# State exponentials and 1/rms without TensorE transposes: VectorE block transposes and DMA in a fused attention and feed-forward kernel

## The chip, the core and the metric

The kernel runs on one core of a Trainium2 chip. A core has a matrix engine (TensorE, "PE" in the profile, with its weight loads as "PEld"), VectorE (DVE), ScalarE (ACT), GpSimd (POOL), a queue engine that issues transfers (SyncE, "SP" or "SPq"), and 16 DMA engines that carry them. The metric is the time of one execution on the device in microseconds, lower is better. The kernel before takes 791.16 us, the median of three runs between 791.04 and 791.2.

## What is computed

Two blocks follow one another. The first is a cross attention between 512 tokens and 32 state vectors, for 8 batches and 8 heads of width 64, in both directions: tokens read from states and states read from tokens. The second is a gated feed-forward layer on all 8 x 544 rows, with a normalization by the root of the mean square (rms) ahead of it. The reference, cut to what matters:

```python
# x: (8, 8, 512, 64)   state: (8, 8, 32, 64)
scores = scale * x @ state.T ;  a  = softmax(scores)       # 512 x 32 for each head
xread  = a @ state                                          # the tokens' rows
scores2 = scale * state @ x.T ; a2 = softmax(scores2)       # 32 x 512 for each head
sread  = a2 @ x                                             # the states' rows
y = concatenate([xread, sread], axis=2)  ->  rows (8*544, 512)
rms = sqrt(mean(y*y, -1) + 1e-6)
yn  = y / rms * rms_g                                       # rms_g: 512 numbers
out = (silu(yn @ w_gate) * (yn @ w_val)) @ w_out            # 512 -> 1536 -> 512
```

All is float32.

## The kernel before

The batches are worked in periods. While TensorE does the two feed-forward products of batch b, the attention of batch b+1 is done beside and between them. Each piece of work is a generator, which yields after every step; one string gives the order in which the generators are stepped, and TensorE, VectorE and ScalarE run their instructions in just this order. Transfers go out on the SyncE queue, in the order in which the program issues them, and SyncE waits at each for whatever that transfer needs.

```python
PERIOD = (
    "hhtvtvhtxhuxhuthhtuhuhtxhhhutuuuhthhuttxahhxhthuuuuuxhavuvhtxhtxhhttuauhxuxhxuut"
    "hhhtuhthutuuhuuuhhauuhtaaauxuhthautuuhhthuhuautaaphuuuapuaaaaacaasapcpaaaaaaaakp"
    "psackaauaacakkpapaakaacpsaskcsssppsasspwswkswxkxxkkpxpxccxss"
)
# h: products to the hidden layer   t, u: their copies (ScalarE) and sums (VectorE)
# p: products of the second layer   c, k: their copies and sums, with the stores
# a: tokens_read(b+1)               s: states_read(b+1)
# w, v: own weights of a batch, two of them for b+1, with the next 1 MB of weights fetched
```

The attention weights of the next batch come from `tokens_read`. Its last steps find 1/rms of each token and scale the weights by it:

```python
    def mean_root(ss, n):
        ri = two.tile([P, NC], F32, name="ri")
        GE.tensor_tensor(out=ri[:, 0:n], in0=ss, in1=mhalf[:, 0:n], op=ALU.pow)     # line 270
        return ri

    def along_rows(ri, n):
        rp = aps.tile([P, NC, P], F32, name="at")
        for c in range(n):
            TE.transpose(out=rp[:, c, :], in_=ri[:, c:c + 1].to_broadcast([P, P]),  # line 277
                         identity=ident)
        return rp.rearrange("p c t -> p (c t)")

    def tokens_read(b):
        ...                                    # softmax over the states, and the read: line 410
        sq = one.tile([P, 4, S], F32, name="sq", tag="xT")
        for i, j in enumerate((2, 3, 0, 1)):
            SE.activation(out=sq[:, i, :], in_=reads[j], func=ACTF.Square, scale=DM ** -0.5)
            ...
        for i, j in ((0, 1), (2, 3), (0, 2)):
            VE.tensor_tensor(out=sq[:, i, :], in0=sq[:, i, :], in1=sq[:, j, :], op=ALU.add)
            yield
        sp = aps.tile([P, NC], F32, name="at")
        for c in range(NC):                                        # NC = 4
            TE.matmul(out=sp[:, c:c + 1], lhsT=sq[:, 0, P * c:P * c + P], rhs=ones,   # line 424
                      start=True, stop=True)
        yield
        ss = two.tile([P, NC], F32, name="ss")
        VE.tensor_scalar(ss, sp, 1e-6, None, op0=ALU.add)          # line 428
        yield "step"
        ri = mean_root(ss, NC)
        yield
        rp = along_rows(ri, NC)
        yield
        VE.tensor_tensor(out=aT_s[b], in0=aT_s[b],                 # line 434
                         in1=rp.unsqueeze(1).to_broadcast([P, 2, S]), op=ALU.mult)
        yield "step"
```

The states' rows come from `states_read`. The exponentials are made with the states on partitions, and are needed with the tokens on partitions:

```python
    def states_read(b):
        ...                                                        # the maxima
        for e in range(2):
            SE.activation(out=e2[:, e], in_=sS[:, e], func=ACTF.Exp, scale=SCALE,
                          bias=s2[:, e:e + 1], accum_out=z2[:, e:e + 1])
            yield "step" if e else None
        e2T = one.tile([P, 2, NC, P], F32, name="e2T")
        for e in range(2):
            tp = aps.tile([P, NC, P], F32, name="at")
            for c in range(NC):
                TE.transpose(out=tp[:, c, :], in_=e2[:, e, c, :], identity=ident)   # line 459
            yield
            SE.copy(e2T[:, e], tp)                                 # line 461
            yield "step"
        ...
        for e in range(2):
            for c in range(NC):
                for j in range(4):
                    h = 2 * j + e
                    TE.matmul(out=rp[Ns * j:Ns * j + Ns, e, :],    # line 471
                              lhsT=e2T[:, e, c, Ns * j:Ns * j + Ns],
                              rhs=xb[:, c, D * h:D * h + D], ...)
        ...                                                        # scaled, transposed, kept
```

The products of the second layer are line 836 (fourteen steps `p` in a period, each 6 matmuls in the program, 12 in the trace, where each float32 matmul of this kind shows as two). A batch's own weights are line 528, and each of them is followed by `fetch`, which issues the load of the next 1 MB of weights. The sums `k` and copies `c` of a period also store eight tiles of 128 KB, through the same SyncE queue.

Of the kernel before, what the change touches and what calls it, by code (L numbers as in the profile page):

```python
# [8 lines left out]
F32 = mybir.dt.float32  # L9
# [3 lines left out]
ALU = mybir.AluOpType  # L13
ACTF = mybir.ActivationFunctionType
AXX = mybir.AxisListType.X
PSUM = bass.MemoryType.PSUM

P = 128
# [10 lines left out]
)  # L29

PERIOD = (
    "hhtvtvhtxhuxhuthhtuhuhtxhhhutuuuhthhuttxahhxhthuuuuuxhavuvhtxhtxhhttuauhxuxhxuut"
    "hhhtuhthutuuhuuuhhauuhtaaauxuhthautuuhhthuhuautaaphuuuapuaaaaacaasapcpaaaaaaaakp"
    "psackaauaacakkpapaakaacpsaskcsssppsasspwswkswxkxxkkpxpxccxss"
)

STATES = (
# [6 lines left out]
def kernel(  # L44
# [20 lines left out]
    nc = tc.nc  # L65
    VE, SE, GE, TE = nc.vector, nc.scalar, nc.gpsimd, nc.tensor
# [50 lines left out]
    def load_x(b, *queues):  # L117
# [8 lines left out]
        for c in range(NC):  # L126
# [3 lines left out]

    ident = consts.tile([P, P], F32, name="ident")
    make_identity(nc, ident)
    mhalf = consts.tile([P, NC], F32, name="mhalf")
    GE.memset(mhalf, -0.5)
    ones = consts.tile([P, 1], F32, name="ones")
    GE.memset(ones, 1.0)

    GE.tensor_tensor(out=consts.tile([P, NC], F32, name="first_pow"), in1=mhalf,
                     in0=ones.to_broadcast([P, NC]), op=ALU.pow)
    bounds = consts.tile([P, 2], F32, name="bounds")  # L140
    GE.memset(bounds[:, 0:1], 1151.0 + 7.5 / 16)
    GE.memset(bounds[:, 1:2], 255.0 * (1 << 23))
    rms_g = consts.tile([P, NI], F32, name="rms_g")


    w_d = [scratch.tile([P, NI, 2, 2, P], F32, name="w_d%d" % mp) for mp in range(NM // 2)]
    w_sb = {}
    wo = consts.tile([P, NM, DM], F32, name="wo")
    hb = consts.tile([P, NM, S], F32, name="hb")
# [117 lines left out]
    def mean_root(ss, n):  # L267

        ri = two.tile([P, NC], F32, name="ri")
        GE.tensor_tensor(out=ri[:, 0:n], in0=ss, in1=mhalf[:, 0:n], op=ALU.pow)  # L270
        return ri
# [11 lines left out]
    def scores(b, packed, soft):  # L283

        xb = x_sb[b]
        stT = two.tile([P, 4, Ns], F32, name="stT")
        tp = aps.tile([P, 4, Ns], F32, name="at")
        TE.transpose(out=tp.rearrange("p j n -> p (j n)"),
                     in_=packed.rearrange("p e d -> p (e d)"), identity=ident)
        yield  # L290
        VE.tensor_copy(stT, tp)
        yield "step"

        xT = one.tile([P, 4, NC, P], F32, name="xT", tag="xT")
        for c in range(NC):
            tp = aps.tile([P, 4, P], F32, name="at")
            for j in range(4):
                TE.transpose(out=tp[:, j, :], in_=xb[:, c, P * j:P * j + P], identity=ident)
            yield
            SE.copy(xT[:, :, c, :], tp)  # L300
            yield "step"
# [12 lines left out]
        eS = soft["e"] = one.tile([P, 2, S // Ns, Ns], F32, name="eS", tag="eS")  # L314
        for e in range(2):
            VE.transpose(out=eS[:, e].rearrange("p k n -> p (k n)"), in_=sp[e])
            yield
            SE.copy(sS[:, e].rearrange("p c t -> p (c t)"), sp[e])
            yield "step" if e else None

        soft["st"] = stT
        soft["half"] = lambda e: eS[:, e]
        soft["back"] = lambda e: [(aT_s[b][:, e], eS[:, e].rearrange("p k n -> p (k n)"))]

    def scores_of_blocks(b, packed, soft):
# [30 lines left out]
        for g in (2, 3, 0, 1):  # L356
# [7 lines left out]
                                   eS[:, g].rearrange("p e c n -> p e (c n)"))  # L364
                                  for g in (2 * q, 2 * q + 1)]

    def tokens_read(b):
        packed, soft = rows.pop(b), {}
        yield from (scores if b < 2 else scores_of_blocks)(b, packed, soft)
        half = soft["half"]  # L370
        m1 = two.tile([P, 2, S // Ns], F32, name="m1")
        z1 = two.tile([P, 2, S // Ns], F32, name="z1")

        def along(t, e):
            return t[:, e].unsqueeze(2).to_broadcast([P, S // Ns, Ns])

        for e in range(2):
            VE.reduce_max(out=m1[:, e], in_=half(e), axis=AXX)
            yield
            VE.tensor_tensor(out=half(e), in0=half(e), in1=along(m1, e), op=ALU.subtract)  # L380
            yield
            SE.activation(out=half(e), in_=half(e), func=ACTF.Exp, scale=SCALE)
            yield "step"
        stT_g[b] = two.tile([P, 4, Ns], F32, name="stT_g")
        if b > 1:
            soft["st"] = aps.tile([P, 4, Ns], F32, name="at")
            TE.transpose(out=soft["st"].rearrange("p j n -> p (j n)"),
                         in_=packed.rearrange("p e d -> p (e d)"), identity=ident)
            yield
        VE.tensor_tensor(out=stT_g[b], in0=soft["st"], in1=rms_g.unsqueeze(2).to_broadcast([P, 4, Ns]),  # L390
                         op=ALU.mult)
        yield
        aT_s[b] = two.tile([P, 2, S], F32, name="aT_s")
        for e in range(2):
            VE.reduce_sum(out=z1[:, e], in_=half(e), axis=AXX)
            yield
            VE.tensor_scalar(z1[:, e], z1[:, e], 1e-9, None, op0=ALU.add)
            VE.reciprocal(z1[:, e], z1[:, e])
            yield
            VE.tensor_tensor(out=half(e), in0=half(e), in1=along(z1, e), op=ALU.mult)  # L400
            yield
            for to, blocks in soft["back"](e):
                VE.transpose(out=to, in_=blocks)
            yield "step"


        reads = [(aps, vps)[j // 2].tile([P, S], F32, name=("at", "pv")[j // 2]) for j in range(4)]
        for j in range(4):
            for e in range(2):
                TE.matmul(out=reads[j][D * e:D * e + D, :],  # L410
                          lhsT=packed[Ns * j:Ns * j + Ns, e, :],
                          rhs=aT_s[b][Ns * j:Ns * j + Ns, e],
# [5 lines that stand above are left out]
            yield "step" if i == 3 else None  # L418
        for i, j in ((0, 1), (2, 3), (0, 2)):
            VE.tensor_tensor(out=sq[:, i, :], in0=sq[:, i, :], in1=sq[:, j, :], op=ALU.add)  # L420
            yield
        sp = aps.tile([P, NC], F32, name="at")
        for c in range(NC):
            TE.matmul(out=sp[:, c:c + 1], lhsT=sq[:, 0, P * c:P * c + P], rhs=ones,  # L424
                      start=True, stop=True)
        yield
        ss = two.tile([P, NC], F32, name="ss")
        VE.tensor_scalar(ss, sp, 1e-6, None, op0=ALU.add)
        yield "step"
        ri = mean_root(ss, NC)  # L430
        yield
        rp = along_rows(ri, NC)
        yield
        VE.tensor_tensor(out=aT_s[b], in0=aT_s[b],  # L434
                         in1=rp.unsqueeze(1).to_broadcast([P, 2, S]), op=ALU.mult)
        yield "step"

    def states_read(b):

        xb, sS = x_sb.pop(b), read.pop(b)  # L440
        e2 = one.tile([P, 2, NC, P], F32, name="e2")
        s2 = two.tile([P, 2], F32, name="s2")
        m2 = two.tile([P, 2], F32, name="m2")
        z2 = two.tile([P, 2], F32, name="z2")
# [4 lines left out]
        VE.tensor_scalar(s2, m2, -SCALE, None, op0=ALU.mult)  # L449
        yield  # L450
        for e in range(2):
            SE.activation(out=e2[:, e], in_=sS[:, e], func=ACTF.Exp, scale=SCALE,
                          bias=s2[:, e:e + 1], accum_out=z2[:, e:e + 1])
            yield "step" if e else None
        e2T = one.tile([P, 2, NC, P], F32, name="e2T")
        for e in range(2):
            tp = aps.tile([P, NC, P], F32, name="at")
            for c in range(NC):
                TE.transpose(out=tp[:, c, :], in_=e2[:, e, c, :], identity=ident)  # L459
            yield  # L460
            SE.copy(e2T[:, e], tp)
            yield "step"
        VE.tensor_scalar(z2, z2, 1e-9, None, op0=ALU.add)
        VE.reciprocal(z2, z2)
        yield
# [1 line left out]
        for e in range(2):  # L467
            for c in range(NC):
                for j in range(4):
                    h = 2 * j + e  # L470
                    TE.matmul(out=rp[Ns * j:Ns * j + Ns, e, :],  # L471
                              lhsT=e2T[:, e, c, Ns * j:Ns * j + Ns],
                              rhs=xb[:, c, D * h:D * h + D],
                              start=(c == 0), stop=(c == NC - 1))
        yield
# [567 lines left out]
```

## Time and profile before

| what | value |
|---|---|
| time, median of 3 | 791.16 us |
| span of the profiled run | 789.0 us, TensorE clock granted 1.000 |
| busy share VectorE, ScalarE, GpSimd | 66%, 42%, 22% |
| share of the 16 DMA engines, SyncE's queue | 36.6% |
| one period (from one batch's line 471 to the next one's, 214.57 and 300.05 us) | 85.48 us |
| transposes of the exponentials, line 459 | 64, mean 273 ns from start to end |
| their copies on ScalarE, line 461 | 16, mean 581 ns |
| sums over partitions, line 424 | 64, mean 241 ns |
| spread of 1/rms, line 277 | 34, mean 274 ns |
| power -1/2 on GpSimd, line 270, 128 x 4 | 8, mean 1692 ns |
| scaling by 1/rms on VectorE, line 434 | 8, mean 1220 ns |

How to read it: matmuls are pipelined, so the time that one of them takes from start to end is longer than the time by which the next one follows. What a group of them costs TensorE is read from the starts in the timeline. Busy shares are averages over the span; the length is set by the engine that has no gaps.

### The profile page before, as it was taken

How to read it: one execution, taken by the hardware profiler on the slowest of the kernel's cores; microseconds unless marked ns; L12 is line 12 of the kernel's file. 1: busy time of each engine (PE TensorE's matmuls, PEld its weight loads, DVE VectorE, ACT ScalarE, POOL GpSimd, SP SyncE). 2: the span in 40 equal slices, each digit the busy share in tenths (PEclk: the TensorE clock that was granted, in tenths of full speed). 3: DMA queues.
4: the chain of work that ended last, by engine and by line, in shares of the span. 5: the costliest groups of instructions: out<-in, count | busy, mean ns of one | idle time of the engine just before them, and what ended most of it. 6: DMA issues, size and time to landing. Idle time of an engine off the chain costs nothing.

```text
span 789.0 us, 13559 instructions
## 1 busy us (share of the span) xinstructions
PE 776.5 (98%) x5478; PEld 603.5 (76%) x5478; DVE 521.5 (66%) x822; ACT 334.4 (42%) x560; POOL 170.9 (22%) x216
## 2 busy tenths in 40 slices
PE   6999999999999999999999999999999999999998
PEld 5643444788877887888878887788788887888996
DVE  4999997688338951897168833895189715781461
ACT  5998864552245323542255224532354225410320
POOL 0100003430244023410433024402341043400000
PEclk9999999999999999999999999999999999999999
DMA  9788865730075005610263008400530034201311
GB/s 286 226 287 298 276 191 167 217 122 1 25 239 181 2 18 181 227 22 17 102 206 121 1 26 257 163 2 15 201 154 7 14 106 149 108 7 34 121 54 27
DMA packets 69277, 95.77 MB, mean 121 GB/s; under 512 B 46432, under 2 KB 54112, under 8 KB 62304
## 3 DMA queue, kind: packets, MB, share of 16 engines
q1 hardware_dynamic: 67040, 94.33, 36.6%
q8 instruction: 43, 0.70, 0.4%
q10 hardware_dynamic: 2176, 0.59, 0.4%
q14 instruction: 18, 0.15, 0.1%
HBM read 79.69 MB, written 15.20 MB: 120 GB/s over the span
## 4 chain that ended last, share of the span: by engine, by line
PE 92%; DVE 5%; DMA 1%; issue 0%; ACT 0%; SPq 0%
PE f L674 37%; PE f L836 35%; PE f L776 5%; PE pv L570 4%; PE at L528 3%; PE pv L528 3%; DVE ex L248 1%; PE at L471 1%; PE at L410 1%; DVE raw L244 1%; PE at L346 1%; PE at L459 1%; PE at L424 1%; DMA raw<-in_moe_w_gate_dram 1%; DVE w_m L253 1%; PE pv L346 1%
## 5 line engine op out<-in xcount | busy, mean ns | idle before, releaser
L836 PE MATMUL f<-wo,hb 128*128 128x256 f32 x540 | 123.4, 380 | 0.2 <-ACT ot L873 0.2
L674 PE MATMUL f<-aT_s,v 128*128 128x256 f32 x504 | 120.6, 382 | 0.0
L836 PEld LDWEIGHTS f<-wo,hb 128*128 128x128 f32 x540 | 101.4, 190 | 13.6 <-ACT ot L873 0.4
L674 PEld LDWEIGHTS f<-aT_s,v 128*128 128x128 f32 x504 | 94.1, 190 | 19.6 <-DVE c L736 5.0
L736 DVE TENSOR_TENSOR g<-g,f 128x512 f32<-128x512 f32 (+1 forms) x96 | 61.8, 653 | 68.4 <-PE f L674 63.9
L674 PE MATMUL f<-aT_t,vs 128*128 128x256 f32 x336 | 87.1, 381 | 0.0
L270 POOL TENSOR_TENSOR ri<-ss,mhalf 128x4 f32<-128x4 f32 x8 | 13.5, 1692 | 320.4 <-DVE s L449 210.9
L727 ACT ACTIVATE hb<-g 128x1024 f32<-128x1024 f32 (+1 forms) x48 | 48.2, 1004 | 79.3 <-DVE g L736 79.3
L836 PE MATMUL f<-wt,hs 128*128 128x256 f32 x360 | 81.0, 381 | 0.0
L836 PEld LDWEIGHTS f<-wt,hs 128*128 128x128 f32 x360 | 67.3, 190 | 14.1 <-issue 5.1
L674 PEld LDWEIGHTS f<-aT_t,vs 128*128 128x128 f32 x336 | 63.2, 190 | 15.0 <-issue 5.9
L873 ACT COPY ot<-f 128x256 f32<-128x256 f32 x60 | 21.4, 373 | 123.0 <-PE f L836 123.0
L554 POOL TENSOR_TENSOR vs<-v 128x256 f32<-128x256 f32 x42 | 31.3, 746 | 164.2 <-ACT v L539 164.1
L739 DVE SCALAR_TENSOR_TENSOR hb<-hb,g 128x1024 f32<-128x1024 f32 x42 | 53.2, 1266 | 4.6 <-ACT hb L727 4.6
L725 ACT COPY g<-f 128x512 f32<-128x512 f32 (+1 forms) x48 | 26.9, 561 | 55.8 <-PE f L674 55.8
L776 PE MATMUL f<-wo,hb 128*128 128x512 f32 x96 | 44.7, 600 | 0.0
L557 POOL TENSOR_TENSOR vs<-v,vs 128x256 f32<-128x256 f32 x42 | 44.4, 1057 | 0.0
L570 PE MATMUL pv<-aT_s,v 128*128 128x512 f32 x96 | 43.7, 594 | 0.2 <-DVE aT_s L434 0.2
L674 PE MATMUL f<-aT_s,vs 128*128 128x256 f32 x168 | 43.1, 379 | 0.0
L674 PE MATMUL f<-aT_t,v 128*128 128x256 f32 x168 | 43.1, 379 | 0.0
L836 PE MATMUL f<-wo,hs 128*128 128x256 f32 x180 | 41.1, 379 | 0.0
L836 PEld LDWEIGHTS f<-wt,hb 128*128 128x128 f32 x180 | 33.7, 190 | 9.4 <-DVE ot L881 5.0
(144 smaller groups left out, 1277.0 us busy)
## 6 DMA issues: line engine op xcount, KB each, us to landing
w_m<-w_d SPq DMA_DIRECT2D x48, 1024.0 KB, 6.5
out_dram<-ot SPq DMA_DIRECT2D x56, 128.0 KB, 2.2
raw<-in_moe_w_val_dram SPq DMA_DIRECT2D x6, 1024.0 KB, 5.5
raw<-in_moe_w_out_dram SPq DMA_DIRECT2D x6, 1024.0 KB, 8.6
x_b<-in_x_dram SPq DMA_DIRECT2D x96, 64.0 KB, 2.8
w_d<-w_m SPq DMA_DIRECT2D x6, 1024.0 KB, 4.9
raw<-in_moe_w_gate_dram SPq DMA_DIRECT2D x5, 1024.0 KB, 7.1
x_b<-in_x_dram SPq DMA_DIRECT2D x6, 256.0 KB, 6.8
```

Source lines behind the costliest of these rows:

```text
L528: TE.matmul(out=pv[e][Ns * j:Ns * j + Ns, :], lhsT=stT_g[b][D * e:D * e + D, j, :], rhs=w[D * e:D * e + D, j].rearrange("p m k f -> p (m k ...
L554: GE.tensor_tensor(out=vs[:, 0], in0=a21, in1=a22, op=ALU.add)
L557: GE.tensor_tensor(out=vs[:, 2], in0=a12, in1=vs[:, 1], op=ALU.subtract)
L570: TE.matmul(out=to[0], lhsT=lhs(i, k), rhs=r, start=(i == 0), stop=(i == len(rhs) - 1))
L674: TE.matmul(out=ps[:, i, 0:half], lhsT=l[:, i, :], rhs=r, start=(start and i == 0 and k == 0), stop=(k == len(lhs) - 1), skip_group_check= ...
L725: SE.copy(gates(q)[1], q["x"][:, :, 0:half])
L727: SE.activation(out=hb[:, 2 * mp:2 * mp + 2, 0:n].rearrange("p m (c t) -> p m c t", c=2), in_=q["g"][:, :, :, 0:half], func=ACTF.Silu if s ...
L736: VE.tensor_tensor(out=to, in0=to, in1=q[ps][:, :, 0:half], op=ALU.add)
L739: VE.scalar_tensor_tensor(out=h, in0=h, scalar=1.0, op0=ALU.add, op1=ALU.mult, in1=q["g"].rearrange("p m c t -> p m (c t)"))
L776: TE.matmul(out=banks[r], lhsT=hb[:, m, P * r:P * r + P], rhs=wo[:, m, :], start=(m == 0), stop=(m == NM - 1))
L836: TE.matmul(out=banks[name][:, r, :], lhsT=lhs(k)[:, P * r:P * r + P], rhs=rhs(k), start=(start and r == 0 and k == 0), stop=(k == HM - 1) ...
L873: SE.copy(to, banks[name][:, r, :])
```

## The change

It concerns batches 2 to 7; batches 0 and 1 keep the code before. Three parts of TensorE's work on the attention are replaced, so that TensorE has more room for its products.

1. The exponentials are written in an order by groups of 32 tokens, transposed by VectorE in blocks of 32 by 32 with one instruction, and 16 transfers carry the blocks from SBUF to SBUF to the partitions where the product of line 471 wants them. Eight transposes by TensorE and two copies by ScalarE fall away.
2. The sums of squares are transposed in blocks by VectorE as well and summed there along the row to 16 columns; one product with a constant matrix sums over the groups. Four products with a column of ones fall away.
3. 1/rms is then held by 32 partitions with 16 columns. One transfer writes it to DRAM, and a second one reads it back to all 128 partitions. Four transposes fall away.

The order of the period is rewritten with it.

```diff
 PERIOD = (
-    "hhtvtvhtxhuxhuthhtuhuhtxhhhutuuuhthhuttxahhxhthuuuuuxhavuvhtxhtxhhttuauhxuxhxuut"
-    "hhhtuhthutuuhuuuhhauuhtaaauxuhthautuuhhthuhuautaaphuuuapuaaaaacaasapcpaaaaaaaakp"
-    "psackaauaacakkpapaakaacpsaskcsssppsasspwswkswxkxxkkpxpxccxss"
+    "hhvtvthhtuxxhuhuhtxhthtuhhuthhuhuuhtuahthutuxxhutuhuhxhttvauxxaxuvhthhhxuuthuhhu"
+    "xuhththuuthuhuutuuhtahxuathtahhhauhtauuuuuuahatuaauuphuupaaaaaaappaappsaaaaaaakc"
+    "acspacuasaakpkaaacacakpcaapskpakkkspsawwxxswkxxpEkcsxspssxc"
 )
 ...
+    groups = consts.tile([P, 4, Ns], F32, name="groups")
+    for i in range(4):
+        GE.tensor_copy(groups[:, i], ident[:, 0:Ns])
+        for j in range(1, 4):
+            GE.tensor_tensor(out=groups[:, i], in0=groups[:, i],
+                             in1=ident[:, Ns * j:Ns * j + Ns], op=ALU.add)
 ...
+    ri_d = [scratch.tile([S // Ns, Ns], F32, name="ri_d%d" % k) for k in range(2)]
 ...
+    def rms_on_blocks(b, sq):
+        n = S // Ns
+        VE.transpose(out=sq[:, 1, :], in_=sq[:, 0, :])
+        yield
+        part = one.tile([P, n], F32, name="part")
+        VE.reduce_sum(out=part, in_=sq[:, 1, :].rearrange("p (k f) -> p k f", f=Ns), axis=AXX)
+        yield
+        sp = aps.tile([P, n], F32, name="at")
+        TE.matmul(out=sp, lhsT=groups.rearrange("p i t -> p (i t)"), rhs=part,
+                  start=True, stop=True)
+        yield
+        ss = one.tile([P, n], F32, name="ssb")
+        VE.tensor_scalar(ss[0:Ns], sp[0:Ns], 1e-6, None, op0=ALU.add)
+        yield "step"
+        ri = one.tile([P, n], F32, name="rib")
+        GE.tensor_tensor(out=ri[0:Ns], in0=ss[0:Ns], in1=mhalf[0:Ns], op=ALU.pow)
+        nc.sync.dma_start(out=ri_d[b % 2].rearrange("k t -> t k"), in_=ri[0:Ns])
+        nc.sync.dma_start(out=sq[:, 2, :],
+                          in_=ri_d[b % 2].rearrange("k t -> (k t)").unsqueeze(0).to_broadcast([P, S]))
+        yield
+        return sq[:, 2, :]
 ...
-        (the sums, the power and the spread shown above)
+        rp = yield from (rms_on_array if b < 2 else rms_on_blocks)(b, sq)
 ...
-        e2 = one.tile([P, 2, NC, P], F32, name="e2")
+        e2 = one.tile([P, 4, 2, NC, Ns], F32, name="e2")
 ...
+            eB = one.tile([P, 4, 2, NC, Ns], F32, name="eB", tag="eS")
+            VE.transpose(out=eB.rearrange("p g e c n -> p (g e c n)"),
+                         in_=e2.rearrange("p g e c t -> p (g e c t)"))
+            for g in range(4):
+                for j in range(4):
+                    nc.sync.dma_start(out=e2T[Ns * g:Ns * g + Ns, j],
+                                      in_=eB[Ns * j:Ns * j + Ns, g])
+            yield
 ...
-                              lhsT=e2T[:, e, c, Ns * j:Ns * j + Ns],
+                              lhsT=(e2T[:, j, e, c, :] if b > 1 else
+                                    flat[:, e, c, Ns * j:Ns * j + Ns]),
```

`groups` has a one wherever row and column agree modulo 32. `rms_on_array` is the code before under a name. A letter of the string that no stream has (`E`) is passed over. What else the diff holds is the rewriting of tiles to these shapes, and one buffer in place of two for the small tile `stT`, which only batches 0 and 1 use.

More of the change, by code (lines that the diff above doesn't have):

```diff
@@ L132 @@
     make_identity(nc, ident)
-    mhalf = consts.tile([P, NC], F32, name="mhalf")
+    mhalf = consts.tile([P, S // Ns], F32, name="mhalf")
     GE.memset(mhalf, -0.5)
@@ L136 @@
     GE.memset(ones, 1.0)
-    GE.tensor_tensor(out=consts.tile([P, NC], F32, name="first_pow"), in1=mhalf,
+    GE.tensor_tensor(out=consts.tile([P, NC], F32, name="first_pow"), in1=mhalf[:, 0:NC],
                      in0=ones.to_broadcast([P, NC]), op=ALU.pow)
@@ L285, in scores @@
         xb = x_sb[b]
-        stT = two.tile([P, 4, Ns], F32, name="stT")
+        stT = one.tile([P, 4, Ns], F32, name="stT")
         tp = aps.tile([P, 4, Ns], F32, name="at")
@@ L365, in scores_of_blocks, with rms_on_array @@
                                   for g in (2 * q, 2 * q + 1)]
+    def rms_on_array(b, sq):
+        sp = aps.tile([P, NC], F32, name="at")
+        for c in range(NC):
+            TE.matmul(out=sp[:, c:c + 1], lhsT=sq[:, 0, P * c:P * c + P], rhs=ones,
+                      start=True, stop=True)
+        yield
+        ss = two.tile([P, NC], F32, name="ss")
+        VE.tensor_scalar(ss, sp, 1e-6, None, op0=ALU.add)
+        yield "step"
+        ri = mean_root(ss, NC)
+        yield
+        rp = along_rows(ri, NC)
+        yield
+        return rp
+    def rms_on_blocks(b, sq):
[7 more added lines that the diff above has]
+        TE.matmul(out=sp, lhsT=groups.rearrange("p i t -> p (i t)"), rhs=part,
+                  start=True, stop=True)
+        yield
+        ss = one.tile([P, n], F32, name="ssb")
+        VE.tensor_scalar(ss[0:Ns], sp[0:Ns], 1e-6, None, op0=ALU.add)
+        yield "step"
+        ri = one.tile([P, n], F32, name="rib")
[3 more added lines that the diff above has]
+                          in_=ri_d[b % 2].rearrange("k t -> (k t)").unsqueeze(0).to_broadcast([P, S]))
+        yield
+        return sq[:, 2, :]
     def tokens_read(b):
@@ L421, in tokens_read @@
             yield
[L422 to L433, printed above, removed]
+        rp = yield from (rms_on_array if b < 2 else rms_on_blocks)(b, sq)
         VE.tensor_tensor(out=aT_s[b], in0=aT_s[b],
@@ L440, in states_read @@
         xb, sS = x_sb.pop(b), read.pop(b)
-        e2 = one.tile([P, 2, NC, P], F32, name="e2")
+        e2 = one.tile([P, 4, 2, NC, Ns], F32, name="e2")
+        exps = e2.rearrange("p g e c t -> p (g e c t)").rearrange("p (e c s) -> p e c s", e=2, s=P)
         s2 = two.tile([P, 2], F32, name="s2")
@@ L451, in states_read @@
         for e in range(2):
-            SE.activation(out=e2[:, e], in_=sS[:, e], func=ACTF.Exp, scale=SCALE,
+            to = e2[:, :, e].rearrange("p g c t -> p c g t")
+            if b < 2:
+                to = exps[:, e]
+            SE.activation(out=to, in_=sS[:, e].rearrange("p c (g t) -> p c g t", t=Ns)
+                          if b > 1 else sS[:, e], func=ACTF.Exp, scale=SCALE,
                           bias=s2[:, e:e + 1], accum_out=z2[:, e:e + 1])
             yield "step" if e else None
[L455 to L459, printed above, removed]
+        e2T = one.tile([P, 4, 2, NC, Ns], F32, name="e2T")
+        if b < 2:
+            flat = e2T.rearrange("p j e c n -> p (j e c n)").rearrange("p (e c s) -> p e c s", e=2, s=P)
+            for e in range(2):
+                tp = aps.tile([P, NC, P], F32, name="at")
+                for c in range(NC):
+                    TE.transpose(out=tp[:, c, :], in_=exps[:, e, c, :], identity=ident)
+                yield
+                SE.copy(flat[:, e], tp)
+                yield "step"
+        else:
+            eB = one.tile([P, 4, 2, NC, Ns], F32, name="eB", tag="eS")
[5 more added lines that the diff above has]
+                                      in_=eB[Ns * j:Ns * j + Ns, g])
             yield
-            SE.copy(e2T[:, e], tp)
-            yield "step"
         VE.tensor_scalar(z2, z2, 1e-9, None, op0=ALU.add)
```

## The prediction

> **What bounds the kernel now.** I read the page's busy shares and slices first, then the list of who waited for whom, then the timeline of TensorE over the end of one period, and last SyncE's. Busy time and waits, from the page and from the waits of TensorE's matmuls:
>
> ```profile
> PE 776.5 (98%) x5478; PEld 603.5 (76%) x5478; DVE 521.5 (66%) x822; ACT 334.4 (42%) x560; POOL 170.9 (22%) x216
> ...
> PE 92%; DVE 5%; DMA 1%; issue 0%; ACT 0%; SPq 0%
> ```
>
> ```profile
> PE at L288 <- DMA rows<-in_state_dram: 6.0, 1, 6.0
> PE at L424 <- DVE sq L420: 1.0, 1, 1.0
> ```
>
> The second line is the chain that ended last: 92% of it is TensorE. The other two are the longest waits of its matmuls: 6.0 us for the first load, then 1.0 us in 789. In the periods nothing holds TensorE up, so time taken from its queue shortens the run by as much, and a new wait in front of it lengthens the run by as much. The change must be read as a trade of these two. Here is TensorE at the end of a period (start, length to the last end, instruction):
>
> ```profile
> 287.39 0.95 PE L424 MATMUL at<-ones,sq 128*128 128x1 f32 x8
> 288.20 2.84 PE L836 MATMUL f<-wo,hb 128*128 128x256 f32 x12
> 290.87 0.60 PE L277 MATMUL at<-ident,ri 128*128 128x128 f32 x4
> 291.31 0.60 PE L459 MATMUL at<-ident,e 128*128 128x128 f32 x4
> 291.75 2.75 PE L836 MATMUL f<-wo,hb 128*128 128x256 f32 x12
> 294.34 2.75 PE L836 MATMUL f<-wo,hs 128*128 128x256 f32 x12
> 296.93 0.60 PE L459 MATMUL at<-ident,e 128*128 128x128 f32 x4
> 297.37 2.75 PE L836 MATMUL f<-wo,hs 128*128 128x256 f32 x12
> 300.05 1.10 PE L471 MATMUL at<-x_b,e2T 128*32 128x64 f32 x64
> 301.08 1.09 PE L528 MATMUL pv<-w_m,stT_g 64*32 64x512 f32 x16
> 301.96 1.06 PE L528 MATMUL at<-w_m,stT_g 64*32 64x512 f32 x16
> 302.96 5.45 PE L836 MATMUL f<-wt,hb 128*128 128x256 f32 x24
> ```
>
> What a group costs is the distance to the next start, not its length: a set of four transposes 0.44 us, the sums 0.81, a step of the second layer 2.59, and 2.67 or 2.68 where it follows a group of another kind. Last, SyncE issuing (its own timeline), the load of rms_g by its tile (least, median and most ns of the issue), and two small loads on the page (KB each, us to landing):
>
> ```profile
> 282.38 1.72 SPq L108 DMA_DIRECT2D rows<-in_state_dram  x4
> ...
> 309.70 7.53 SPq L122 DMA_DIRECT2D x_b<-in_x_dram  x15
> ```
>
> ```profile
> L954 SPq DMA_DIRECT2D rms_g<-in_moe_rms_g_dram x1: 1032/1032/1032, 4.2 to 4.2; - x1
> ```
>
> ```profile
> rows<-in_state_dram SPq DMA_DIRECT2D x32, 16.0 KB, 1.8
> ...
> rms_g<-in_moe_rms_g_dram SPq DMA_DIRECT2D x1, 2.0 KB, 4.1
> ```
>
> The reader is to see that issuing alone costs SyncE 1.72/4 = 0.43 us a transfer for small ones and 7.53/15 = 0.50 for those of 64 KB, and that a transfer of 512 single numbers (rms_g, 128 x 4) took 1.03 us to issue and 4.1 to land.
>
> **What the Trainium skill says.** "VectorE: DVE Perf Modes", The three transpose paths: VectorE transposes in blocks of 32 by 32 only, TensorE the full 128 by 128 into PSUM. That is why the change needs transfers after VectorE. The trace has the VectorE form already (128 x 1024 in 1.235 us, line 335). "DMA: Bandwidth & Descriptors", Two DMAs through the same engine are not ordered: a transfer that reads what another wrote must be issued only after the first one's completion has been waited for. So SyncE must stand between the write of 1/rms and its read; no transfer of the kernel before reads so soon after a write, so this trace doesn't show it. The same page, Anatomy of one DMA, puts the fixed cost of a transfer at about 2.0 us, most of it until the write is confirmed; the trace agrees with 1.8 us for 16 KB. "Perfetto Trace Analysis", What "DMA-bound" means, names the issuing engine's sequencer as a bound of its own; the pitch of 0.43 to 0.50 us above is that bound at work.
>
> **The change part by part, on TensorE.** Per batch it loses the sums (0.81), the spread of 1/rms (0.44), two sets of transposes (0.88) and two of the slower starts after them (0.08 and 0.09): 2.30 us. It gains the one product with `groups`: two passes at the 0.10 us each that line 424's passes take (0.81/8), and a slower start, 0.28. Line 471 now stands between two steps of line 836, another slower start, 0.10. Net 2.30 - 0.38 = 1.92 us, times 6 batches = 11.5 us, which is 1.5% of the time.
>
> On ScalarE two copies of 0.58 us go. VectorE gains a block transpose of 128 x 512 (0.69, line 316), a sum along 512 (0.66, line 395) and a block transpose of 128 x 1024 (1.24): 2.6 us in a period of 85.48, at 66% busy. These lie beside TensorE. The two VectorE steps ahead of the product with `groups` have room: TensorE has three steps of line 836, 7.9 us, between line 410 and that product, against some 4.0 us from line 410 to the last sum of squares (281.5 + 0.6 to 286.1) plus 1.35.
>
> **The new chain.** I take the end of the product with `groups` as zero and follow TensorE's order in the changed program: a step of line 836 (2.67), two more (5.18), two sets of own weights (1.02 and 0.86 by their starts, 301.08 to 302.96 in all), a step (2.68), then line 471. TensorE arrives there at 12.4 us. The 16 transfers' data is due then. SyncE's order is: write 1/rms, read it, two stores, the 16 transfers. Its clock:
>
> - VectorE's sum and the power: started 0.42 after line 424 ended (288.20 to 288.62), 1.74 long at 4 columns. With 16 columns on 32 partitions I guess 2.1, so 2.5.
> - The write: 32 x 16 single numbers, the same 512 as rms_g. Issued at about 2.65; rms_g's 4.1 us came while the queues were full at the start, so I take 3.1: landed 5.8.
> - The read (0.45) and two stores (0.4 each): SyncE free at 7.15. VectorE's block transpose is done well before, near 4.7: it follows the two sums of line 881, which wait for the step that ends at 2.7.
> - 16 issues: at 0.45 the last goes out at 7.15 + 15 x 0.45 = 13.9 and lands 1.8 later, at 15.7.
>
> So TensorE waits 15.7 - 12.4 = 3.3 us. The four matmuls at the head of line 471 use the four blocks of the last group of partitions, so its start can't slip ahead of the last transfers. Six such waits, one for each of batches 2 to 7, are 19.8 us. Sum: 791.2 - 11.5 + 19.8 = 799.5; I say 799.
>
> Behind it, the next load of weights leaves SyncE after the 16 issues, near 14.4, some 1.3 us ahead of line 471, and is used 6.3 us into what follows (line 471 1.03, a step 2.69, a transpose 0.11, two products 1.5, the first own weights 1.0): 7.7 us for 1 MB, whose median landing is 6.1 for this tile, at most 9.4. In the kernel before it had 311.06 - 302.49 = 8.6. This should just hold. The scaling by 1/rms is ready at about 5.9 + 2 + 1.2 = 9.1, ahead of its first use after line 471.
>
> **Rivals.** (1) All transfers hidden: if the write of 1/rms lands in 2 us and issues go at 0.35 us, the last one lands near 13, and only the 11.5 us less a little remain: about 780 to 783. For it: small transfers do land in 1.8 us, and the order of the period was made anew with room in it. Against it: no stretch of SyncE in this trace issues faster than 0.43. (2) The late load of weights becomes a second wait: 1 to 2 us per batch more, about 808. For it the maximum of 9.4 us; against it that the 16 transfers have landed by then and the queues are empty. (3) VectorE's order: it waits in its queue for 1/rms before the sums that store, and a delay there could hold the next period's first products. The sums of line 881 need TensorE's step at 7.9 and come at about 9.5; nothing needs them before 12.4. It would cost nothing or a few tenths.
>
> **Range and chances.** The gain on TensorE is firm to half a microsecond per batch. The wait is the open term: issue pitch 0.40 to 0.50 (14.5 +- 0.8 for the last), the write 2 to 4 us, together a wait between about 1 and 5.5 us. That gives 785 to 812. Faster by over 2% would need 775.3, below even the case without any wait, so 0.03. Slower by over 2% is 807, a wait of 4.6: 0.16. Within: 0.81.
>
> **What would show it.** The counterparts of lines 277, 424 and 459 with about a quarter of their counts; TensorE idle some 3 us six times, at line 471, put down to a transfer into `e2T`; SyncE issuing 16 transfers in some 7 us, and standing 2 to 4 us before the read of 1/rms. It would be wrong if line 471 started with no wait (then near 780), if TensorE waited elsewhere (for weights at line 584 of the changed kernel, or for line 471's scale), or if the write of single numbers took far longer than rms_g.

## The result, and the profile after

The changed kernel takes 868.45 us (median of four runs, 867.02 to 870.89) against 791.18 us before: a ratio of 1.098, with a 95% interval of 1.095 to 1.100. It is slower by 77 us, or 12.9 us for each of the six batches that the change concerns. The prediction said 799, and 785 to 812.

In the changed kernel the lines are numbered anew: 526 is the states' product (471 before), 892 the second layer (836), 730 the hidden layer's products (674), 584 the own weights (528), 929 the copies of the second layer's banks (873; a bank is a buffer into which TensorE writes products and which another engine then copies out). The page, with busy shares, the clock granted to TensorE in 40 slices, and the chain that ended last:

```profile
PE 790.6 (91%) x5370; PEld 603.8 (69%) x5370; DVE 539.7 (62%) x840; ACT 327.7 (38%) x548; POOL 186.6 (21%) x232
...
PEclk9999999999699988999699997999699997999999
...
PE 78%; SPq 7%; DMA 6%; DVE 4%; POOL 4%; issue 1%; ACT 0%; DVEq 0%; POOLq 0%
```

The longest waits of TensorE's matmuls (us in all, times, longest):

```profile
PE at L526 <- DMA e2T<-eB: 62.0, 18, 10.9
...
PE f L892 <- ACT ot L929: 5.0, 13, 0.5
```

TensorE was 98% busy and is now 91%. The chain that was 92% TensorE is 78%, and SyncE, the transfers and GpSimd have come into it. Most of that is one wait, some 10.3 us in each batch, at the place that the prediction named. Two things stand beside it that it did not name: the clock row has a dip in each period, and TensorE waits for a copy by ScalarE at line 892.

TensorE's timeline over one such end of a period:

```profile
204.34 0.29 PE L401 MATMUL at<-part,groups 128*128 128x16 f32 x2
204.97 2.86 PE L892 MATMUL f<-wo,hb 128*128 128x256 f32 x12 [0.33 <-ACT ot L929]
207.66 5.34 PE L892 MATMUL f<-wo,hs 128*128 128x256 f32 x24
212.93 1.09 PE L584 MATMUL pv<-w_m,stT_g 64*32 64x512 f32 x16
213.81 1.06 PE L584 MATMUL at<-w_m,stT_g 64*32 64x512 f32 x16
214.81 2.86 PE L892 MATMUL f<-wt,hb 128*128 128x256 f32 x12
227.58 0.39 PE L526 MATMUL at<-x_b,e2T 128*32 128x64 f32 x2 [9.91 <-DMA e2T<-eB]
...
230.30 1.92 PE L526 MATMUL at<-x_b,e2T 128*32 128x64 f32 x58
232.15 3.77 PE L892 MATMUL f<-wt,hb 128*128 128x256 f32 x12
235.76 0.27 PE L538 MATMUL at<-ident,sr 128*128 128x128 f32 x1
```

The product with `groups` ends near 204.6, TensorE is at the states' product at 217.5, and stands until 227.6. What it does then is slow as well: the step of line 892 at 232.15 takes 3.6 us to the next start in place of 2.7. The chain that it waits for, in the timelines of GpSimd and of SyncE:

```profile
204.91 4.42 POOL L408 TENSOR_TENSOR rib<-ssb,mhalf 32x16 f32<-32x16 f32 x1 [39.09 <-DVE ssb L405]
```

```profile
209.36 0.31 SPq L409 DMA_DIRECT2D ri_d<-rib  x1
215.75 0.34 SPq L410 DMA_DIRECT2D sq<-ri_d  x1
216.18 1.69 SPq L959 DMA_DIRECT2D out_dram<-ot  x2
217.95 10.11 SPq L515 DMA_DIRECT2D e2T<-eB  x16
```

SyncE issues the write of 1/rms at 209.36 and then nothing for 6.4 us: its next instruction reads what is being written. VectorE's block transpose had ended at 208.53 + 1.24 = 209.77, so the data of the 16 transfers lay ready for 8 us behind a queue that stood for something else.

Clock and busy time in three stretches of the same place, and in four shorter ones within them (stretch, length, busy time of each engine, granted clock, share and rate of the DMA engines):

```profile
217.50:227.50 10.00, 0.17 (x1) 0.00 (x0) 2.12 (x5) 0.86 (x2) 5.92 (x9) 0.64 0.38 95
227.50:236.00 8.50, 7.96 (x80) 5.97 (x81) 0.48 (x2) 0.04 (x1) 2.45 (x4) 0.62 0.77 274
236.00:245.00 9.00, 9.00 (x66) 6.51 (x65) 3.52 (x5) 5.04 (x9) 2.98 (x4) 1.00 0.59 147
217.70:220.00 2.30, 0.00 (x0) 0.00 (x0) 0.00 (x0) 0.86 (x2) 0.00 (x0) 1.00 0.80 199
222.00:224.00 2.00, 0.00 (x0) 0.00 (x0) 0.21 (x1) 0.00 (x0) 1.92 (x4) 0.50 0.19 49
233.00:234.00 1.00, 1.00 (x3) 0.75 (x3) 0.00 (x0) 0.00 (x0) 0.00 (x0) 0.50 1.03 352
235.00:235.80 0.80, 0.80 (x6) 0.65 (x5) 0.00 (x0) 0.00 (x0) 0.00 (x0) 1.00 0.86 342
```

The clock is 0.64 in the wait, still 0.62 in the 8.5 us of work after it, and 1.00 only then. These are means. The four short stretches show two levels: 1.00 at the start of the wait, 0.50 in the rest of it and until about 234, that is 6.4 us after TensorE had begun to work again, then 1.00. The clock was already at 0.50 when the DMA engines moved 49 GB/s, and was back at 1.00 at 342.

### The profile page after: what moved, and what is told of

Same layout as the page of the kernel before. It is cut to its first block, busy times and chain, and to the rows that moved or that the text cites. A ratio compares the mean times of both kernels' runs of the same rounds, so it can differ in the third digit from the quotient of the medians.

```text
span 868.9 us, 13549 instructions
## 1 busy us (share of the span) xinstructions
PE 790.6 (91%) x5370; PEld 603.8 (69%) x5370; DVE 539.7 (62%) x840; ACT 327.7 (38%) x548; POOL 186.6 (21%) x232
## 4 chain that ended last, share of the span: by engine, by line
PE 78%; SPq 7%; DMA 6%; DVE 4%; POOL 4%; issue 1%; ACT 0%; DVEq 0%; POOLq 0%
PE f L730 35%; PE f L892 25%; SPq L515 6%; DMA ri_d<-rib 5%; PE f L832 4%; PE pv L626 4%; POOL rib L408 3%; PE at L584 2%; PE pv L584 2%; PE at L526 2%; DMA e2T<-eB 1%; DVE ex L256 1%; PE at L458 1%; SPq L959 1%; PE at L354 1%
## 5 line engine op out<-in xcount | busy, mean ns | idle before, releaser
L730 PE MATMUL f<-aT_s,v 128*128 128x256 f32 x504 | 123.5, 389 | 0.0
L526 PE MATMUL at<-x_b,e2T 128*32 128x64 f32 x512 | 20.9, 289 | 62.0 <-DMA e2T<-eB 62.0
L408 POOL TENSOR_TENSOR rib<-ssb,mhalf 32x16 f32<-32x16 f32 x6 | 26.6, 4425 | 234.8 <-DVE ssb L405 234.8
L610 POOL TENSOR_TENSOR vs<-v 128x256 f32<-128x256 f32 x42 | 33.5, 796 | 149.7 <-ACT v L595 149.7
L526 PEld LDWEIGHTS at<-x_b,e2T 128*32 128x32 f32 x512 | 15.2, 153 | 71.9 <-issue 69.8
L795 DVE SCALAR_TENSOR_TENSOR hb<-hb,g 128x1024 f32<-128x1024 f32 x42 | 55.8, 1329 | 7.2 <-ACT hb L783 7.2
L892 PE MATMUL f<-wt,hb 128*128 128x256 f32 x180 | 48.2, 423 | 0.0
L471 DVE TENSOR_TENSOR aT_s<-aT_s,sq 128x1024 f32<-128x1024 f32 x6 | 7.3, 1225 | 61.6 <-DMA sq<-ri_d 61.6
L892 PEld LDWEIGHTS f<-wt,hb 128*128 128x128 f32 x180 | 37.3, 214 | 11.5 <-issue 6.0
```

The source lines that it names most:

```text
L408: GE.tensor_tensor(out=ri[0:Ns], in0=ss[0:Ns], in1=mhalf[0:Ns], op=ALU.pow)
L526: TE.matmul(out=rp[Ns * j:Ns * j + Ns, e, :], lhsT=(e2T[:, j, e, c, :] if b > 1 else flat[:, e, c, Ns * j:Ns * j + Ns]), rhs=xb[:, c, D * ...
L610: GE.tensor_tensor(out=vs[:, 0], in0=a21, in1=a22, op=ALU.add)
L730: TE.matmul(out=ps[:, i, 0:half], lhsT=l[:, i, :], rhs=r, start=(start and i == 0 and k == 0), stop=(k == len(lhs) - 1), skip_group_check= ...
L795: VE.scalar_tensor_tensor(out=h, in0=h, scalar=1.0, op0=ALU.add, op1=ALU.mult, in1=q["g"].rearrange("p m c t -> p m (c t)"))
L892: TE.matmul(out=banks[name][:, r, :], lhsT=lhs(k)[:, P * r:P * r + P], rhs=rhs(k), start=(start and r == 0 and k == 0), stop=(k == HM - 1) ...
```

## The experiments

The theory after the result: TensorE waits for a chain in which SyncE's order ties two independent things together, and the lower clock follows from the waiting. The rivals: 16 small transfers are late by themselves; 1/rms is late by itself; the clock falls for another reason, such as the traffic that lands then.

**One part alone: e2 and e3.** In e2 the states' part stays as changed and 1/rms goes over TensorE as before; in e3 it is the other way round. Both keep the changed order of the period.

```diff
 e2:  -   rms_on_blocks(b, sq)     +   (sums on `ones`, power, along_rows, as before)
 e3:  -   eB, 16 transfers         +   8 TE.transpose, 2 SE.copy into e2T, as before
```

> Part 1 of the change alone, in the order of period of the changed kernel: the states' exponentials by VectorE's blocks and 16 transfers, but the sums of squares and 1/rms on TensorE as before. Theory A (the 16 transfers are late mainly because they queue behind the write and the read of 1/rms on SyncE): they start at 5.7 us after the sums' product instead of 13.3, end near 17.8, TensorE comes at about 13.5: a wait of 4 to 4.5 us in place of 10.4, total 814 to 830 us, the upper end if the clock still drops. Rival B (16 issues alone are the cause, whatever stands before them): wait 8 us and more, 845 us and above.

> Parts 2 and 3 alone, in the order of period of the changed kernel: 1/rms by blocks, a write to and a read from DRAM, but the states' exponentials transposed on TensorE. Theory A (1/rms itself arrives just in time for the next period's first product, some 17 us after the product with groups; only what GpSimd makes of it is late by 2 to 3 us): 800 to 812 us, with short waits of TensorE at the next period's first products and no drop of the clock. Rival B (the round trip of 1/rms alone costs most of the loss): 840 us and above. Rival C (it is hidden): 786 to 790.

Measured: e2 819.5 us (ratio 1.035, 1.032 to 1.038), as expected in time. The 16 transfers now start when their data are there, but still take SyncE 10.3 us to issue:

```profile
211.97 10.34 SPq L531 DMA_DIRECT2D e2T<-eB  x16
```

TensorE comes near 220.6 and waits about 2 us in four pieces, half of what was expected, with a lower clock after them. e3 took 815.8 us (1.030, 1.027 to 1.033), above the 812 expected. The waits of TensorE in e3:

```profile
PE at L588 <- DMA w_m<-w_d: 7.4, 6, 1.6
PE f L734 <- POOL vs L614: 6.9, 6, 1.2
```

The second of them was foreseen, GpSimd's sums that start when 1/rms has been multiplied in. The first is the late load of weights that the prediction had as a rival. In this trace VectorE stands for 1/rms until 221.67, and in its order the sums that store come behind; SyncE stands for those stores (218.08 to 224.33) and issues the weights at 224.42. Each part alone costs 24 to 27 us. Together they cost 77, more than their sum. The next run tests whether that is because one is queued behind the other.

**Only the queue of 1/rms: e6.**

```diff
-        nc.sync.dma_start(out=ri_d[b % 2]...)
+        nc.gpsimd.dma_start(out=ri_d[b % 2]...)
-        nc.sync.dma_start(out=sq[:, 2, :], ...)
+        nc.gpsimd.dma_start(out=sq[:, 2, :], ...)
```

> The changed kernel with the write and the read of 1/rms issued from GpSimd's queue in place of SyncE's; nothing else differs. Theory A (the 16 transfers are late because SyncE, in order, waits for the write's landing before the read): they start at about 5.5 us after the product with groups in place of 13.3, the last lands near 17.8, TensorE comes at 12.9: a wait near 5 in place of 10.4 us, total 834 us, 822 to 842. Rival B (the order on the queue doesn't matter, the 16 transfers are late by their own issues or by what the engines carry): 855 and above. Rival C (1/rms itself becomes the bound, as GpSimd's transfers take longer): the wait moves to the first products of the next period.

Measured: 830.3 us (1.049, 1.047 to 1.051). No work was taken away, and 38 us of the 77 are gone. SyncE's and TensorE's lines:

```profile
210.62 11.96 SPq L515 DMA_DIRECT2D e2T<-eB  x16
```

```profile
PE at L526 <- DMA e2T<-eB: 24.0, 11, 4.9
```

The transfers start at 210.6 in place of 218.0, and the wait falls from 62.0 to 24.0 us. The write itself is no faster from this queue (6.4 us to landing). So half of the loss is the order on one queue.

**Why the write takes so long: e4.** One more block transpose turns 1/rms from 32 partitions with 16 numbers each to 16 with 32, so that each partition's numbers lie in one run in DRAM. In the order of the period one sum of the second layer changes places with one step of `tokens_read`, so that two stores go out between the write and the read.

```diff
-        nc.sync.dma_start(out=ri_d[b % 2].rearrange("k t -> t k"), in_=ri[0:Ns])
+        VE.transpose(out=sq[0:Ns, 3, Ns:2 * Ns], in_=sq[0:Ns, 3, 0:Ns])
+        nc.sync.dma_start(out=ri_d[b % 2], in_=sq[0:n, 3, Ns:2 * Ns])
 ...
 the end of the period, with the number of each step
- p11 a41 k6 k7 k8
+ p11 k6 a41 k7 k8
```

> The changed kernel with 1/rms turned by one more 32 x 32 block transpose on VectorE ahead of its write, so that the write has 16 runs of 128 bytes in place of 512 single numbers. Two stores move ahead of the read by it. Theory A (the 6.4 to 7.6 us of this write come from its single numbers): it lands in about 2 us, the chain is some 5.5 us shorter, TensorE's wait about 5 in place of 10.4: 826 to 840 us. Rival B (a round trip to DRAM takes that long whatever its runs): the write still takes over 5 us, 858 us and above.

Measured: 834.8 us (1.054, 1.051 to 1.057), as expected. The write in the changed kernel, and then in e4 (KB, median us to landing):

```profile
ri_d<-rib SPq DMA_DIRECT2D x6, 2.0 KB, 6.8
```

```profile
ri_d<-sq SPq DMA_DIRECT2D x6, 2.0 KB, 1.3
```

The same 2 KB land in 1.3 us as 16 runs of 128 bytes, and in 6.8 us as 512 runs of 4 bytes. The runs are the cause of the write's length, and not the trip to DRAM. The 34 us that e4 is faster than the changed kernel are the shorter write and the new place of the two stores together.

**The clock: e1 and e5.** TensorE multiplies constants while it would wait, 22 times or 28 times.

```diff
+        if b > 1:
+            idle = vps.tile([P, 2, P], F32, name="pv")
+            for i in range(FILL):                      # 22 in e1, 28 in e5
+                TE.matmul(out=idle, lhsT=ident, rhs=ident.unsqueeze(1).to_broadcast([P, 2, P]),
+                          start=True, stop=True)
```

> The changed kernel with 22 products of constants on TensorE (ident by ident, 256 columns, result unused) ahead of the states' product of each of batches 2 to 7, about 0.43 us each, 9.5 us in all: they fill most of the 10.4 us in which TensorE waits for the transfers into e2T. Theory A (the lower granted clock after the wait is a consequence of TensorE's standing idle): the clock stays near 1.0, the states' product and the step of the second layer after it take their 1.0 and 2.6 us again, 3.8 us less per batch, so 868 - 6 x 3.8 = 845 us, 840 to 850. Rival B (the lower clock comes from something else, such as the transfers that land at that time): no change or longer, 866 to 872, with the clock still low.

Measured: 864.7 us (1.092, 1.089 to 1.095), far from the 845 expected. The filler was too short. The clock stayed at 1.00 in three of the six periods, the first, second and last, where two to four gaps of 0.3 to 0.5 us were left, at most 1.3 us in all. It fell to a mean of 0.77 in the other three. The third and fourth had a first gap of 1.5 us and three of 0.3; the fifth had four gaps of 0.3 to 0.5 us, 1.5 us in all. The clock over the states' product and the step after it, in the first, the third and the fifth period:

```profile
228.80:234.40 5.60, 4.60 (x77) 3.72 (x78) 0.48 (x2) 0.00 (x0) 2.67 (x4) 1.00 0.68 239
422.50:429.90 7.40, 6.29 (x78) 4.95 (x79) 0.47 (x2) 0.00 (x0) 2.82 (x5) 0.77 0.76 255
620.20:627.70 7.50, 6.29 (x77) 4.96 (x78) 0.48 (x2) 0.00 (x0) 2.97 (x5) 0.77 0.76 250
```

The stretches carry nearly the same traffic (239, 255 and 250 GB/s), and the first has no low clock. A period that kept its clock was 96.0 to 96.6 us long, one that did not 98.4 to 99.4 (from one product with `groups` to the next). That speaks against the traffic. The next run was to settle it.

> The run with 22 filler products again, with 28 of them: 12.1 us of constants' products per batch, more than the wait they cover. With 22 the clock kept up in two of the six periods and fell in four, where 1.5 us and some 0.3 us gaps were left. Theory A (the granted clock falls where TensorE stands idle for a good part of a few microseconds): no gap is left, no drop in any period; a period is then 85.5 - 1.9 + 0.8 + 12.1 = 96.5 us in place of 98.0, 857 us (853 to 861), faster than with 22 although it does more. Rival B (the drop has another cause): 6 x 2.6 us more work and the drop stays, 875 to 882.

Measured: 860.6 us (1.087, 1.085 to 1.090). The expectation counts two periods of e1 that kept the clock and four that lost it; the trace of e1 has three and three. Six more products per batch, and the time is 4 us shorter, not 16 longer. TensorE then has no wait at line 532 (the states' product in this run), and the mean granted clock of the whole run is 1.000, against 0.992 with 22 and 0.953 to 0.961 in the changed kernel. The same place, in the first such period:

```profile
230.70:235.30 4.60, 4.60 (x82) 4.02 (x82) 0.77 (x3) 0.37 (x1) 0.00 (x0) 1.00 0.98 365
```

The clock is 1.00 in all six, at 321 to 365 GB/s. So the low clock was a consequence of TensorE's standing. It fell for less than one long gap: in e1, gaps of 0.3 to 0.5 us that came to 1.5 us were enough once, and gaps that came to 1.3 us were not. No run shows where the limit lies.

**The issue time: e7.** As e2, with half of the 16 transfers on ScalarE's queue.

```diff
-                    nc.sync.dma_start(out=e2T[...], in_=eB[...])
+                    (nc.scalar if (4 * g + j) % 4 < 2 else nc.sync).dma_start(out=e2T[...], in_=eB[...])
```

> Part 1 alone, as in the run e2 (1/rms on TensorE), with 8 of the 16 transfers issued by ScalarE and 8 by SyncE. Theory A (what was left of the wait in e2, some 2 us and the drop of the clock after it, is the issue time of 16 transfers on one queue, 10.3 us): two queues take 5.2 us each, the last lands near 219 where TensorE comes at 220.6, no wait and no drop: 786 to 792 us, against 819.5 for one queue. Rival B (16 small transfers from SBUF to SBUF hold each other up whatever queue issues them): 805 and above.

Measured: 796.3 us (1.0054, 1.0037 to 1.0071), between the two expectations. SyncE's half and ScalarE's half:

```profile
211.35 5.05 SPq L531 DMA_DIRECT2D e2T<-eB  x8
```

```profile
211.35 6.01 ACTq L531 DMA_DIRECT2D e2T<-eB  x8
```

Issuing on two queues takes 5 to 6 us in place of 10.3, and takes 23 us from the time. The wait for the transfers is 0.8 us once and none in the other periods. It was still 4.5 us slower than the kernel before. Two places in its trace show where: 0.46 us at line 908 (the second layer), for ScalarE's copy of the bank, and some 0.5 us inside the own weights, which take 1.52 us to the next start (215.81 to 217.33) where they took 1.00. The trace does not name what they wait for.

**All of it mended, and the part that pays: e8 and e9.** e8 is e4 with 12 transfers issued by ScalarE and 4 by SyncE, and with an order in which the product with `groups` comes a step of the second layer earlier, and the exponentials and their block transpose two steps earlier. e9 is part 1 alone in that order, with 1/rms over TensorE.

```diff
 the end of the period, with the number of each step
- c5 a38 k4 p9 c6 a39 a40 p10 s4 k5 p11 a41 k6 k7 k8 s5 p12 s6 a42
+ c5 a38 a39 k4 c6 a40 p9 s4 s5 k5 k6 p10 s6 a41 p11 k7 k8 p12 a42        (e8)
+ c5 a38 a39 k4 c6 a40 p9 s4 s5 k5 k6 p10 s6 a41 p11 a42 k7 k8 p12        (e9)
```

> The whole change, mended: the write of 1/rms in 16 runs (as in e4), 12 of the 16 transfers issued by ScalarE and 4 by SyncE, and the order of the period changed so that the product with groups comes one step of the second layer (2.6 us) earlier and the states' exponentials and block transpose two steps earlier. Theory A (the waits are all of the loss, and the 1.9 us per batch that TensorE saves are real): transfers land near 13.5 us after the product with groups, TensorE comes at 15.1; no wait, clock 1.0, 791 - 11.5 + some waits for copies = 779 to 785 us. Rival B (the freed time on TensorE goes elsewhere): 788 to 795, as before. Rival C (something of the chain is still late): above 795, with waits at the states' product or at the next period's first products.

> Part 1 alone with the order of the mended kernel e8: 12 of the 16 transfers on ScalarE's queue and 4 on SyncE's, the sums of squares on TensorE right ahead of the step whose bank ScalarE is copying, the spread of 1/rms one step of the second layer earlier. Theory A (in e8 the sums' 0.81 us were no gain, as TensorE then stands for the copy of the bank that they covered, so that part 1 and the spread of 1/rms are all that is won): a batch saves 0.9 us, 786 to 787.5 us, some 2 us above e8. Rival B (what e7 lost against the kernel before, +4.5 us, belongs to part 1 itself and not to its place in the period): 793 to 797 as in e7.

Measured: e8 784.3 us (0.991, 0.990 to 0.993), e9 787.1 us (0.994, 0.993 to 0.996). Both are faster than the kernel before, by 0.9% and 0.6%. e8 changes the runs, the queues and the order together, and no run tells what each of them gives. e9 has no wait at the two places where e7 lost time. TensorE in e8, in the second such period:

```profile
286.53 0.36 PE L401 MATMUL at<-part,groups 128*128 128x16 f32 x2
287.13 5.45 PE L892 MATMUL f<-wo,hb 128*128 128x256 f32 x24 [0.24 <-ACT ot L929]
292.42 5.34 PE L892 MATMUL f<-wo,hs 128*128 128x256 f32 x24
297.69 1.09 PE L584 MATMUL pv<-w_m,stT_g 64*32 64x512 f32 x16
298.57 1.06 PE L584 MATMUL at<-w_m,stT_g 64*32 64x512 f32 x16
299.57 2.86 PE L892 MATMUL f<-wt,hb 128*128 128x256 f32 x12
302.35 1.10 PE L526 MATMUL at<-x_b,e2T 128*32 128x64 f32 x64
```

The states' product starts without a wait and at full clock, and a period takes 302.35 - 217.88 = 84.47 us against 85.48. That is 1.0 us saved, not 1.9. Most of the reason stands in the first two lines, beside the same place in e9:

```profile
287.17 0.95 PE L397 MATMUL at<-ones,sq 128*128 128x1 f32 x8
288.07 5.45 PE L908 MATMUL f<-wo,hb 128*128 128x256 f32 x24
```

In e9 the four sums take 0.90 us to the next start (288.07 - 287.17), and no wait follows. In e8, 24 products started at 280.95 and took 5.28, as such a set does (297.69 - 292.42 = 5.27), so they ended at 286.23; the next step starts at 287.13. That is 0.90 us again, though the product with `groups` is far smaller. TensorE must write the bank that ScalarE is still copying, and the sums were work that covered that copy. Taking them away gained nothing. The 2.8 us between e9 and e8 are about what the spread of 1/rms took, 0.44 us six times (2.6).

## Why the prediction was wrong

The direction was right, and so was the mechanism of the main wait: the place, the order on SyncE, the six times. What failed is the size of the wait, 3.3 us predicted and 10.3 measured: four terms of the new chain's sum were too small, all on the same side. One effect, the clock, and one loss, the bank, were missing.

- **The chain's clock.** From the product with `groups` to the last landing it said 15.7 us. The pieces measured are these. The power took 4.42 us for 2.1 guessed. The write took 6.39 from its issue to the read's (209.36 to 215.75), for 3.15. The read and two stores held SyncE 2.20 (215.75 to 217.95) for 1.35. The 16 issues came every 0.635 us (10.11 for 16 of about 0.59 each, with the gaps between) for 0.45. Only the landing of one of them was right: 1.9 for 1.8. The four excesses are 2.3, 3.2, 0.85 and 15 x 0.185 = 2.8, together about 9 us. The wait grew by 7, as TensorE came 0.5 us later and did the first six products of the place while the last transfers landed.
- **The power.** The guess added 0.4 us for 12 more columns. In the kernel before, 2 columns (1.62) and 4 (1.69) differ by little. From 4 to 16 columns it was (4.42 - 1.69)/12 = 0.23 us for one. The two shapes differ in partitions too, 128 and 32, and no run separates the two.
- **The write.** The analogue was the right one and was talked down. rms_g, with 512 single numbers, took 4.1 us as a load, and I took 3.1 for a store because the queues would be empty. e4 shows that single numbers are the cost, and a store of them takes more than the load did. This is the last of the signs of being wrong that the prediction named.
- **The issues.** I took the pitch from transfers out of DRAM. Those from SBUF to SBUF take 0.59 us each by themselves. Rival (1), that all is hidden, fell for that and for the write. In e8, with two queues, the write in runs and the earlier start, it came true, but at 784.3 us and not 780 to 783, for the reason under "The gain on TensorE".
- **TensorE's arrival** at the states' product was right, 12.9 us for 12.4; the rest is a wait for the bank.
- **Missing: the clock.** "The Trainium skill", page "TensorE: Matmul & The Clock Gate", HAM oscillation, says that a wait of TensorE beyond some 3.4 us throttles its clock and that the work after it starts slow. The prediction did not use it. From 227.58 to 235.76, without the gaps, the states' product and the work after it took 7.7 us, against 4.2 for the same work in e5 (1.03, 2.70 and 0.43): 3.6 us in each batch. The trace agrees with the page on a long wait (0.50 after one of 10 us); e1 shows a drop for shorter ones too, 1.5 us in four pieces.
- **The gain on TensorE.** 1.92 us a batch was too much by 0.9. The step that failed is "it loses the sums (0.81)": in e8 the slot of the product with `groups` takes 0.90 us, for the 0.28 predicted. That is 0.6 of the 0.9; the rest, some 0.3 us in a period, was not traced. The profile before showed no wait after them, since they were what filled it. There the sums (287.39 to the next start at 288.20) lie over this copy by ScalarE, which ends at 287.96:

```profile
287.59 0.37 ACT L873 COPY ot<-f 128x256 f32<-128x256 f32 x1 [2.96 <-PE f L836]
```

In the changed kernel the waits for copies at line 892 are 5.0 us in all. e2, with the sums back in the same order, has 3.0 of them, seven waits of at most 0.5 us, so that 2.0 come from the sums' removal and the rest from the new order.
- **Small errors of the working.** They change nothing in the result. By its own terms SyncE is free at 7.05 and not 7.15; the two sets of own weights are 0.88 and 1.00 us by their starts (the sum is right); the two products before the next own weights take 1.83 us and not 1.5 (308.35 to 310.18 in the kernel before).

The sum of one batch, then: -1.9 for the work removed, 10.3 for the states' product, 3.6 for the clock, 0.8 for the copies, 12.8 us. Measured are 12.9 by the medians. Rival (2), the late weights, did not show in the changed kernel, where TensorE came to the next own weights 9 us after the issue of the load (228.17 to 237.26). It showed in e3. Rival (3), VectorE's order, was said to cost nothing or a few tenths; it is what made the weights late in e3. There the read of 1/rms landed after 3.9 us, for the 2 assumed.

## What to carry to other kernels

Before work is moved off a busy engine by transfers, follow the issuing queue as an engine with its own order: sum the issues at the pitch of their own kind, and ask what stands behind each wait in it. Two independent chains on one queue, one of them with a write that is read back, cost more than the two alone, and another queue, or longer runs in the write with another place for two stores, took away about half of the loss without changing the products. And a piece of work that is removed ahead of a buffer's reuse saves only what the copy of that buffer does not then take.

## What the runs showed of the hardware

- A store of 2 KB to DRAM took 6.4 to 7.6 us to land as 512 single numbers and 1.3 us as 16 runs of 128 bytes.
- A transfer of 32 KB from SBUF to SBUF took its issuing queue about 0.59 us, on SyncE as on ScalarE, and landed in 1.9 (in e6, where 1/rms went over another queue, in 3.6). Sixteen in a row took SyncE 10.1 to 10.3 us, and 5.1 and 6.0 on two queues with eight each.
- GpSimd's power took 4.42 us for 32 partitions x 16 numbers and 1.69 for 128 x 4.
- TensorE's clock fell from 1.00 to 0.50 within a 10 us wait and was at 1.00 again after 6.4 us of work. In e1 it fell after four gaps of 0.3 to 0.5 us (1.5 us in all) as well. Constants' products in the wait kept it at 1.00, and the kernel was shorter for them (860.6 us for 868.45).
